# Attention and channel mixing on one Trainium2 core: statistics of the first x tiles ahead of the transposes' copies, and products placed in a wait for a load

## The chip, the cores and the metric

The kernel runs on one core of a Trainium2 chip. The metric is the time of one execution on the device, in microseconds (us); lower is better. Whole times are medians of several runs, with the lowest and highest in brackets where they are given; everything read from a trace is one execution. Engine names in the profile: PE is the matmul engine (TensorE), PEld its weight loads, DVE is VectorE, ACT is ScalarE, POOL is GpSimd, SP the queue that issues most transfers.

## The reference

```python
# batch 8, heads 8, seq 576, head_dim 64, 32 memory slots, d_model 512
a = exp(phi - max(phi, axis=seq));  a = a / (sum(a, axis=seq) + 1e-9)
k_m = einsum('bhsm,bhsd->bhmd', a, k)
v_m = einsum('bhsm,bhsd->bhmd', a, v)
attn = softmax(q @ k_m.T / sqrt(64))            # over the 32 slots
x = (attn @ v_m) laid out as [batch, seq, 512]
xn = (x - mean(x)) / sqrt(var(x) + 1e-6) * g
out = x + relu(xn @ w1) @ w2                    # w1 512x2048, w2 2048x512
```

## The kernel before

Batches are worked off one after the other, and two batches form a pair of 1152 rows, which gives nine tiles of 128 rows. The step of an even batch finishes four of them (`t[0]` to `t[3]`), that of an odd batch five. A step begins with the hidden layer of batch b (`mm1`, tile `h_ps`), then runs the second product tile by tile (`mm2`, tile `ch_ps`, two halves of 8 matmuls per tile), and between those halves it does the attention of the next batch: `a_kv` (memory keys and values), `a_tr` (their transposes), `a_sc` (scores), `a_w1b`, `a_den`. The accumulators lie in PSUM, in two kinds of buffers:

```python
def big(shape, dtype, name):      # two banks each
    return psum.tile(shape, dtype, name=name, tag="big", bufs=3)

def one(shape, dtype, name):      # one bank each
    return psum.tile(shape, dtype, name=name, tag="one", bufs=2)
```

The functions that the change moves:

```python
def x_stats(pr, t):               # VectorE: mean and variance of one x tile
    ...
    nc.vector.bn_stats(out=stt, in_=x)
    nc.vector.bn_aggr(out=mv[:, i, :], in_=stt)

def x_rstd(pr, ts):               # ScalarE: 1/sqrt(var + eps) as Ln and Exp
    ...
    nc.scalar.activation(out=rstd[:, 0:n], in_=mv[:, 0:n, 1], func=AF.Ln, bias=eps_sb)
    nc.scalar.activation(out=rstd[:, 0:n], in_=rstd[:, 0:n], func=AF.Exp, scale=-0.5)

def mm2(pr, t, j0, j1, ...):      # PE: products of one tile into a one-bank buffer
    if j0 == 0:
        chs[(pr, t)] = one([P, C], FP32, "ch_ps")
    ...

def mm2_out(pr, t):               # VectorE: x = ch * rstd + x, frees that buffer; then two writes
    nc.vector.scalar_tensor_tensor(out=x, in0=ch_ps, scalar=rstd, in1=x,
                                   op0=ALU.mult, op1=ALU.add)
    ...
```

The step, cut to what matters (`half(i)` is 8 product matmuls; three tiles in flight need three one-bank buffers, and there are two, so `half(4)`, which opens the third tile, needs `mm2_out(t[0])`):

```python
half(0)
a_kv(nb)                                  # kv_ps; ends with a reciprocal on VectorE (line 232)
x_tiles(pr, t[0:2], False); x_tiles(pr, t[2:4], False)
...
half(1)
a_tr(nb)                                  # kvT: two PSUM copies on VectorE
x_stats(pr, t[0]); x_stats(pr, t[1])
...
half(2)
a_sc(nb)                                  # scores; their exponentials on ScalarE
x_rstd(pr, t[0:2])
a_w1b(nb, 0)                              # evicted by VectorE
mm2_out(pr, t[0])
half(3)
a_den(nb, finish=False)
mm2_out(pr, t[1])
...
half(4)
a_den2(nb)
if odd:
    x_tiles(pr, t[4:5], False)            # fifth tile, four small matmuls
...
```

Batch 1 has a prologue of its own, whose q is transposed on PE in two halves as its load arrives:

```python
mm2(0, 2, 8, 12)
a_tr(1)
a_qT(1, 0)            # 10 transposes into a big buffer, first half of q
a_qT(1, 1)            # 10 transposes, second half of q
a_w1b(1, 0)
mm2(0, 2, 12, 16)     # last four products of tile 2, then mm2_out of tile 2
a_w1b(1, 1)
a_sc(1)
mm2(0, 3, 0, 4)
a_w1b(1, 2)
a_den(1)
...                   # then mm1(1), the first step of the loop
```

The softmax here doesn't subtract the row's maximum and nothing guards it: scores larger than these inputs give would overflow.

## Time and profile before

| | before |
|---|---|
| time, us | 253.18 (253.05 to 253.28, 3 runs) |
| span of the profiled run, us | 251.4 |
| PE busy | 94% |
| idle of PE before `qT_ps` of batch 0 and 1, waiting for the q load | 1.6 us, of which 0.91 in batch 1 |
| idle of PE before `ch_ps`, waiting for `mm2_out` | 1.5 us in six steps |

A timeline row gives the start, the duration, the engine and line, the instruction with its output and input and their shapes, how many were run together, and in brackets the idle time just before it and what ended that. A "releaser" is only the event that came last.

```profile
70.28 1.48 ACT L313 ACTIVATE E_sb<-sc_ps,rs 128x640 bf16<-128x640 f32 x2 [2.30 <-PE sc_ps L308]
71.64 0.29 ACT L445 ACTIVATE rstd<-mv,eps_sb 128x2 f32<-128x2 f32 x1
71.97 0.20 ACT L446 ACTIVATE rstd<-rstd 128x2 f32<-128x2 f32 x1
```

### The profile page before, as it was taken

What the parts mean: (1) busy time and instruction counts of PE and PEld (TensorE: products, weight loads), DVE (VectorE), ACT (ScalarE), POOL (GpSimd) and SP (SyncE); (2) the same over time, 40 slices, a digit from 0 to 9 for tenths busy, and PEclk for the clock granted to TensorE, in tenths of its full rate; (3) what the DMA queues carried; (4) which work ended last, traced back from release to release, by engine and by line L of the source; (5) the groups of instructions that cost most, each with busy time, mean ns of one, the idle gap of its engine ahead of it and who ended that gap; (6) DMA issues with size and microseconds to landing.
All of it is one profiled execution on the core that took longest, in us unless ns stands there. A gap on an engine that the chain in (4) does not pass through costs nothing.

```text
span 251.4 us, 5829 instructions
## 1 busy us (share of the span) xinstructions
PE 236.0 (94%) x2446; PEld 131.6 (52%) x2477; DVE 155.1 (62%) x300; ACT 130.1 (52%) x219; POOL 60.0 (24%) x99
## 2 busy tenths in 40 slices
PE   7878999899999999999999999999999999999993
PEld 2443555447534665367534674467444764476453
DVE  3236773595397655787479646885679537873641
ACT  3154662677364464837382646655581755465220
POOL 8643231027204502090206302270205010000000
PEclk9999999999999999999999999999999999999999
DMA  7999999999996798739973998539892300303133
GB/s 148 192 206 207 206 257 215 282 212 128 211 193 128 130 256 182 146 53 202 249 147 89 142 252 136 123 43 223 200 188 44 78 8 0 86 16 71 44 81 83
DMA packets 41922, 36.82 MB, mean 146 GB/s; under 512 B 17444, under 2 KB 37160, under 8 KB 41896
## 3 DMA queue, kind: packets, MB, share of 16 engines
q0 software_dynamic: 17248, 19.53, 45.8%
q1 hardware_dynamic: 24488, 16.79, 29.2%
q8 instruction: 19, 0.31, 0.5%
q10 hardware_dynamic: 160, 0.13, 0.2%
q14 instruction: 7, 0.06, 0.1%
HBM read 41.42 MB, written 9.44 MB: 202 GB/s over the span
## 4 chain that ended last, share of the span: by engine, by line
PE 72%; DMA 17%; ACT 5%; DVE 2%; issue 2%; POOL 1%; POOLq 0%
PE ch_ps L459 41%; PE h_ps L390 22%; DMA q_bf<-in_q_dram 7%; DMA w2b<-in_moe_w_ch_dram 6%; ACT E_sb L313 4%; DMA kv_bf<-in_k_dram 3%; PE w1b_ps L369 2%; PE o_ps L420 2%; DVE x_sb L483 2%; PE kv_ps L205 2%; PE last_ps L471 1%; PE sc_ps L308 1%; POOL q_bf L92 1%; ACT rstd L446 1%; ACT rstd L445 0%
## 5 line engine op out<-in xcount | busy, mean ns | idle before, releaser
L459 PE MATMUL ch_ps<-w2b,rT 128*128 128x512 bf16 x531 | 123.4, 379 | 3.9 <-issue 1.7
L459 PEld LDWEIGHTS <-rT 128*128 128x128 bf16 x560 | 52.2, 98 | 64.5 <-issue 7.8
L390 PE MATMUL h_ps<-Eh,w1b 128*128 128x288 bf16 x512 | 66.7, 285 | 0.7 <-ACT rT L396 0.5
L396 ACT ACTIVATE rT<-h_ps 128x576 bf16<-128x576 f32 x88 | 52.5, 648 | 27.4 <-PE h_ps L390 27.3
L390 PEld LDWEIGHTS <-w1b 128*128 128x128 bf16 x512 | 49.6, 97 | 17.2 <-issue 2.0
L373 DVE SCALAR_TENSOR_TENSOR w1b<-m_sb,rsum,w1b_ps 128x512 bf16<-128x512 f32 x64 | 43.8, 743 | 6.4 <-PE w1b_ps L369 3.5
L398 DVE TENSOR_SCALAR rT<-h_ps 128x576 bf16<-128x576 f32 x40 | 30.3, 758 | 26.9 <-PE h_ps L390 26.3
L483 DVE SCALAR_TENSOR_TENSOR x_sb<-ch_ps,rstd,x_sb 128x512 f32<-128x512 f32 x35 | 25.6, 744 | 8.6 <-PE ch_ps L459 6.9
L426 ACT ACTIVATE x_sb<-o_ps 128x1024 f32<-128x1024 f32 (+1 forms) x20 | 17.8, 933 | 18.4 <-PE o_ps L420 18.4
L439 DVE BATCH_NORM_STATS2 bst<-x_sb 128x6 f32<-128x512 f32 x36 | 24.3, 676 | 3.1 <-ACT x_sb L426 3.1
L189 POOL TENSOR_TENSOR es<-e_sb 128x512 f32<-128x512 bf16 x6 | 6.9, 1156 | 68.1 <-ACT e_sb L182 68.1
L313 ACT ACTIVATE E_sb<-sc_ps,rs 128x640 bf16<-128x640 f32 x16 | 11.8, 790 | 19.5 <-PE sc_ps L308 19.5
L276 POOL TENSOR_TENSOR vb<-v,vmask 128x256 bf16<-128x256 bf16 x12 | 7.7, 662 | 57.3 <-DVE rs L232 57.3
L445 ACT ACTIVATE rstd<-mv,eps_sb 128x2 f32<-128x2 f32 (+1 forms) x20 | 5.9, 296 | 27.3 <-DVE mv L440 27.3
L355 DVE SCALAR_TENSOR_TENSOR Eh<-E_sb,rs,rden 128x576 bf16<-128x576 bf16 x16 | 12.4, 816 | 8.1 <-ACT rden L354 8.1
L174 PE MATMUL w_ps<-fill 128*128 128x512 f32 x14 | 9.8, 819 | 1.6 <-DVE fill L119 1.6
L369 PE MATMUL w1b_ps<-w1r,kvT 64*32 64x512 bf16 x256 | 10.7, 381 | 0.0
L222 DVE CAST k<-kv_ps 128x256 bf16<-128x256 f32 x7 | 3.0, 424 | 12.5 <-PE kv_ps L205 12.5
L182 ACT ACTIVATE e_sb<-phi_st 128x1152 bf16<-128x1152 f32 x8 | 9.2, 1152 | 2.7 <-DMA phi_st<-in_phi_dram 2.7
L354 ACT ACTIVATE rden<-rden 128x576 f32<-128x576 f32 x16 | 10.0, 673 | 0.1
L261 DVE COPY kvT<-kvT_ps 128x256 bf16<-128x256 bf16 x8 | 2.3, 292 | 12.2 <-PE kvT_ps L259 11.8
L92 POOL DMA_DIRECT2D q_bf<-in_q_dram x10 | 7.6, 761 | 4.6 <-DMA w2b<-in_moe_w_ch_dram 1.9
(73 smaller groups left out, 155.1 us busy)
## 6 DMA issues: line engine op xcount, KB each, us to landing
out_dram<-x_sb SPq DMA_DIRECT2D x70, 128.0 KB, 3.5
kv_bf<-in_k_dram POOLq DMA_DIRECT2D x7, 576.0 KB, 8.8
kv_bf<-in_v_dram POOLq DMA_DIRECT2D x7, 576.0 KB, 12.5
phi_st<-in_phi_dram SPq DMA_DIRECT2D x6, 576.0 KB, 10.5
q_bf<-in_q_dram POOLq DMA_DIRECT2D x6, 576.0 KB, 14.9
w1r<-in_moe_w_ch_dram POOLq DMA_DIRECT2D x4, 512.0 KB, 14.2
w2b<-in_moe_w_ch_dram POOLq DMA_DIRECT2D x4, 512.0 KB, 18.8
q_bf<-in_q_dram POOLq DMA_DIRECT2D x4, 288.0 KB, 12.7
```

The lines of the kernel that those rows point to most:

```text
L92: nc.gpsimd.dma_start(out=t.rearrange("p j n x -> p j (n x)")[:, js, 0:NS * D], in_=rows(q, b)[:, js, :])
L313: nc.scalar.activation(out=E_[:, g].rearrange("p (a x) -> p a x", a=2), in_=sc[:, :, 0:HP], func=AF.Exp, scale=s["rs"][:, g:g + 1])
L355: nc.vector.scalar_tensor_tensor(out=Eh[:, g, :], in0=s["E"][:, g, 0:S], scalar=s["rs"][:, g:g + 1], in1=rd[:, g].rearrange("p a x -> p (a ...
L369: nc.tensor.matmul(ps[32 * j:32 * (j + 1), g, :], s["kvT"][r:r + 64, 2, 32 * j:32 * (j + 1)], w1r[r:r + 64, j, fs], start=True, stop=True, ...
L373: nc.vector.scalar_tensor_tensor(out=s["w1b"][:, g, fs], in0=m_sb[:, fs], scalar=s["rsum"][:, g:g + 1], in1=ps[:, g, :], op0=ALU.mult, op1 ...
L390: nc.tensor.matmul(h_ps[:, half, 0:HS], s["w1b"][:, g, P * j:P * (j + 1)], s["Eh"][:, g, HS * half:HS * (half + 1)], start=(g == 0), stop= ...
L396: nc.scalar.activation(out=dst, in_=h_ps[:, :, 0:HS], func=AF.Relu)
L398: nc.vector.tensor_scalar(out=dst, in0=h_ps[:, :, 0:HS], scalar1=0.0, scalar2=None, op0=ALU.max)
L426: nc.scalar.activation(out=x[:, 0:n].rearrange("p i (u y) -> p i u y", u=2), in_=o_ps.rearrange("p u (i y) -> p i u y", i=2)[:, 0:n], func ...
L439: nc.vector.bn_stats(out=stt, in_=x)
L459: nc.tensor.matmul(ch_ps, rT[:, j, P * t:P * (t + 1)], w2b[:, j, :], start=(j == 0), stop=(j == JC - 1))
L483: nc.vector.scalar_tensor_tensor(out=x, in0=ch_ps, scalar=rstd, in1=x, op0=ALU.mult, op1=ALU.add)
```

## The change

It wants to free the first tile's product buffer earlier in each step (`x_stats`, `x_rstd` and `mm2_out` of the first tile move forward), to put the fifth tile's small matmuls next to the other small ones, and to give PE work in the wait for q in batch 1. For that last part the second q half is put into two one-bank buffers, copied half by ScalarE and half by VectorE. The whole diff:

```diff
--- before.py
+++ after.py
@@ -287,12 +287,21 @@
             nc.sync.dma_start_transpose(out=qTs[b].rearrange("p j n x -> p (j n) x"),
                                         in_=q_bf.rearrange("p j n x -> p (j n x)"))
             return
-        q_ps = big([P, 2, 1024], BF16, "qT_ps")
+        split = b == 1 and i == 1
+        if split:
+
+            qs = [one([P, 1024], BF16, "qT_ps") for _ in range(2)]
+        else:
+            q_ps = big([P, 2, 1024], BF16, "qT_ps")
+            qs = [q_ps[:, u, :] for u in range(2)]
         for u in range(2):
             for n in range(NP):
-                nc.tensor.transpose(q_ps[:, u, P * n:P * (n + 1)], q_bf[:, 2 * i + u, n, :], ident)
+                nc.tensor.transpose(qs[u][:, P * n:P * (n + 1)], q_bf[:, 2 * i + u, n, :], ident)
         dst = qTs[b][:, 2 * i:2 * i + 2].rearrange("p a n x -> p a (n x)")
-        if i == 0 or b == 1:
+        if split:
+            nc.scalar.activation(out=dst[:, 0], in_=qs[0][:, 0:NP * P], func=AF.Copy)
+            nc.vector.tensor_copy(out=dst[:, 1], in_=qs[1][:, 0:NP * P])
+        elif i == 0 or b == 1:
             nc.scalar.activation(out=dst, in_=q_ps[:, :, 0:NP * P], func=AF.Copy)
         else:
             nc.vector.tensor_copy(out=dst, in_=q_ps[:, :, 0:NP * P])
@@ -555,9 +564,9 @@
     mm2(0, 2, 8, 12)
     a_tr(1)
     a_qT(1, 0)
+    mm2(0, 2, 12, 16)
     a_qT(1, 1)
     a_w1b(1, 0)
-    mm2(0, 2, 12, 16)
     a_w1b(1, 1)
     a_sc(1)
     mm2(0, 3, 0, 4)
@@ -601,23 +610,24 @@
             a_kv(nb)
         x_tiles(pr, t[0:2], False)
         x_tiles(pr, t[2:4], False)
+        if odd:
+            x_tiles(pr, t[4:5], False)
         if nb + 1 < B:
             phis[nb + 1] = load_phi(nb + 1)
             load(nb + 1)
         half(1)
+        x_stats(pr, t[0])
+        x_stats(pr, t[1])
+        x_rstd(pr, t[0:2])
         if more:
             a_tr(nb)
-        x_stats(pr, t[0])
-        x_stats(pr, t[1])
         if nb + 1 < B:
             a_qT(nb + 1, 0)
+        mm2_out(pr, t[0])
         half(2)
         if more:
             a_sc(nb)
-        x_rstd(pr, t[0:2])
-        if more:
             a_w1b(nb, 0)
-        mm2_out(pr, t[0])
         half(3)
         if more:
             a_den(nb, finish=False)
@@ -629,9 +639,7 @@
         half(4)
         if more:
             a_den2(nb)
-        if odd:
-            x_tiles(pr, t[4:5], False)
-        else:
+        if not odd:
             a_w1b(nb, 1)
             a_w1b(nb, 2)
             a_w1b(nb, 3)
```

After the change, lines from the second q half on have numbers that are 9 higher: the product is line 468 instead of 459, `mm2_out` 492 instead of 483, `w1b`'s eviction 382 instead of 373.

## The prediction

> **What bounds the kernel now.** I read the page's busy table first, then the waits of the matmul engine, then its timeline beside those of the weight loads and of VectorE.
>
> ```profile
> PE 236.0 (94%) x2446; PEld 131.6 (52%) x2477; DVE 155.1 (62%) x300; ACT 130.1 (52%) x219; POOL 60.0 (24%) x99
> PE ch_ps L459 <- issue: 1.7, 11, 0.2
> PE qT_ps L293 <- DMA q_bf<-in_q_dram: 1.6, 2, 0.9
> ...
> PE ch_ps L459 <- DVE x_sb L483: 1.5, 6, 0.3
> ```
>
> PE is the bound. The waits view (what waited, for whom, us in total, times, longest) lists about 10 us of PE waiting in all, so no reordering of other engines can give much. The change aims at two lines: the q wait of batch 1 (0.91 us, the longest of its two) and the six waits for line 483, `mm2_out`. The "issue" line is not time to win: its 11 gaps of 0.16 us stand where a run of 8 matmuls shows only 7 records, so a record is missing.
>
> Next, one odd step (b=1), PE, then weight loads, then VectorE (start, duration, instruction, idle before and its releaser):
>
> ```profile
> 65.46 0.75 PE L420 MATMUL o_ps<-vb,Eh 64*64 64x128 bf16 x20
> ...
> 72.32 0.44 PE L339 MATMUL den_ps<-E_sb,blk 64*64 64x288 bf16 x8
> 73.01 0.59 PE L459 MATMUL ch_ps<-w2b,rT 128*128 128x512 bf16 x2 [0.25 <-DVE x_sb L483]
> ```
>
> ```profile
> 72.69 0.10 PEld L459 LDWEIGHTS <-rT 128*128 128x128 bf16 x1 [0.23 <-issue]
> 73.01 0.96 PEld L459 LDWEIGHTS <-rT 128*128 128x128 bf16 x5 [0.23 <-issue]
> ```
>
> ```profile
> 66.12 0.16 DVE L232 RECIPROCAL rs<-kv_ps 128x2 f32<-128x2 f32 x1
> 68.25 0.29 DVE L261 COPY kvT<-kvT_ps 128x256 bf16<-128x256 bf16 x1 [1.97 <-PE kvT_ps L259]
> ...
> 70.63 1.41 DVE L373 SCALAR_TENSOR_TENSOR w1b<-m_sb,rsum,w1b_ps 128x512 bf16<-128x512 f32 x2
> 72.20 1.41 DVE L483 SCALAR_TENSOR_TENSOR x_sb<-ch_ps,rstd,x_sb 128x512 f32<-128x512 f32 x2 [0.17 <-ACT rstd L446]
> ```
>
> The third tile's product needs the PSUM bank of the first tile, and VectorE frees it only at 72.20 + 0.75 = 72.95. The weights were loaded at 72.69, and the matmul starts at 73.01. Where nothing is awaited, the first matmul starts with its weight load (70.48 and 70.49 in the same step). So the wait costs 73.01 - 72.69 = 0.32 us, a little more than the printed 0.25, since modelled matmul ends overlap. VectorE is late only because of its order: it sat idle for 1.97 us before the kvT copy, while the statistics, which could have run then, came after it.
>
> **What the Trainium skill says.** "TensorE: Matmul & The Clock Gate", in Architectural detail, says that PE can pull weight loads ahead of matmuls in flight, and that ACT and DVE are strict FIFO. The trace agrees on both: the load at 72.69 ahead of its matmul, and the idle 1.97 us with ready work behind. "Perfetto Trace Analysis", Identifying the Most-Contended Engine, warns that busy share of matmuls is a poor measure; I therefore use starts, not busy time. "TensorE: Matmul & The Clock Gate", Back-to-back issue gap, gives N/2.4 + 2.5, about 216 ns for 512 columns; the trace agrees (8 products take 1.73 us on the chain of waits, 0.216 each). "PSUM — Partial Sum Buffer", Terms, has 8 banks. Here 3 two-bank tiles and 2 one-bank tiles use all of them, so any new allocation waits for an older one.
>
> **Part 1, statistics first (steps b=1 to 6).** Nothing is added, VectorE and ScalarE are reordered. New VectorE order, by durations of the rows above: first x tile evicted at 66.03 + 1.02 = 67.05; two statistics with aggregates, 68.86 to 70.54 before, so 1.69 us: done 68.8. kvT copies (0.29 + 0.28, overlapping) done by 69.3. PE needs kvT at 69.87, so the copies, though later by 0.7 us, still make it with 0.5 us to spare. ScalarE has the reciprocal deviations by 69.4, `mm2_out` of tile 0 ends near 70.2, and the bank is free 2.5 us early. The next waits there (scores' Exp, den, the later w1b buffers) are set by PE's own earlier work; in even steps the third w1b buffer comes free at about 104.3, and PE would arrive at 104.46. So the whole wait goes: 6 x 0.32 = **-1.9 us**.
>
> **Part 2, the fifth tile's `x_tiles` moves up (odd steps).** Its 4 matmuls cost 75.05 - 74.73 = 0.32 us where they stand now, between two products (last product starts 74.52, the next would at 74.73), because of the switch to and from a quarter-array shape. Beside the other o_ps matmuls they cost about 0.14 us. But the built program shows a new wait: as fourth big PSUM tile in a row they take the slot of kv_ps, and wait for the reciprocal of line 232. That ends at 66.28, plus 0.05 for the release = 66.33, against 66.0 for the last o_ps matmul. So the next product starts at 66.33 + 0.07 + 0.14 = 66.55, where it now starts at 66.16: +0.39 there, -0.32 at the old place, **+0.07** in b=1, 3 and 5. The last step has no kv_ps: **-0.17**. Sum about 0.0.
>
> **Part 3, the prologue of batch 1.** Four products (4 x 0.216 = 0.86 us) go into the 0.91 us q wait, which looks like -0.9. I do not believe it, by two terms:
>
> ```profile
> 46.66 0.73 PE L293 MATMUL qT_ps<-ident,q_bf 128*128 128x128 bf16 x10 [0.91 <-DMA q_bf<-in_q_dram]
> 47.32 0.41 PE L369 MATMUL w1b_ps<-w1r,kvT 64*32 64x512 bf16 x8
> 47.66 1.04 PE L459 MATMUL ch_ps<-w2b,rT 128*128 128x512 bf16 x4
> 48.63 0.41 PE L369 MATMUL w1b_ps<-w1r,kvT 64*32 64x512 bf16 x8
> 48.86 0.74 PE L308 MATMUL sc_ps<-qT,kvT 64*32 64x320 bf16 x16
> 49.75 0.59 PE L459 MATMUL ch_ps<-w2b,rT 128*128 128x512 bf16 x2 [0.16 <-issue]
> ```
>
> ```profile
> 47.80 1.41 DVE L373 SCALAR_TENSOR_TENSOR w1b<-m_sb,rsum,w1b_ps 128x512 bf16<-128x512 f32 x2 [2.02 <-PE w1b_ps L369]
> ```
>
> First, the second one-bank q tile takes the bank of the very product that was moved. The four products start at 45.59 and their result is complete at about 46.66; line 483 takes 0.75, so the bank is free at 47.41 and the last five transposes start at 47.46, not 47.0. Second, the second score tile waits, before as after, for the eviction of the first w1b buffer: now 47.80 + 1.41 = 49.21, and the weight loads of the second score tile start at 49.26. VectorE is therefore the path here, not PE. After, VectorE copies the q half (estimate 0.5 us from 0.82 for twice the size) from 47.95 to 48.45, and evicts w1b from 48.37 to 49.77. The second score tile starts at 49.83 instead of 49.27, **+0.56**. From there PE has the same work left; it recovers some 0.15 us, since its wait before the second den tile (for the second w1b eviction) disappears, and gives part back in the first h_ps, which needs Eh, itself 0.5 later. Net **+0.45 us**, with -0.3 to +0.7 thinkable.
>
> **Sum**: -1.9 + 0.0 + 0.45 = -1.4 us; 253.18 - 1.4 = **251.8 us**, -0.6%.
>
> **The rivals.** (a) The intent holds in full: -0.9 in the prologue, -1.9 in the steps, -0.5 from tile five without a new wait: 249.9 us. Against it: the two PSUM slots above, which the built program's waits name. (b) The statistics delay kvT so that scores wait, a wait in the place of the one removed: it needs the 0.5 us margin to be eaten in the odd steps, where ScalarE's third eviction also queues. Since statistics need only the first eviction, I think it unlikely; 0.2 us in each of six steps would make it 253.0. (c) DMA takes the gain: the loads of a batch are issued a step ahead, and the waits view has only 0.2 us for kv_bf in PE's matmuls, so a PE that is 0.3 us faster in each step of 26 to 30 us does not catch up with them. (d) The prologue costs more than 0.7 us because the q half lands later; then 252.3.
>
> **Range and chances.** The repeats of before spread by 0.23 us. The steps' gain is the surest term, 1.5 (six times the printed 0.25) to 1.9; the prologue and part 2 carry some 0.5 us each way. 251.0 to 252.7 should hold 8 times in 10. A 2% move is 5 us, half of all PE waits listed, and in the other direction nothing comes near: same 0.985, faster 0.01, slower 0.005.
>
> **What would show it.** PE's waits for line 483 before the third tile are gone, the first product after den starts with its weight load, and the period of an even step (84.73 to 110.47, 25.74 us) drops to about 25.4, of an odd one (29.64) to about 29.4. A new PE wait of 0.1 to 0.3 us for VectorE's line 232 stands at the fifth tile in three odd steps. In the prologue PE waits near 47.0 for line 483 (instead of 46.6 for DMA), and again about 1 us before the second score tile; the first h_ps of b=1 starts near 55.0, not 54.52. Wrong would be: kvT waits in the steps, or a first h_ps before 54.3.

## More of the kernel before

ScalarE was idle for 2.30 us until the scores came. It then did the two exponentials of the scores and only after them the two tiny instructions of the reciprocal deviation (`rstd`), which therefore was ready at 72.17. VectorE's `mm2_out` needs it.

## The result, and the profile after

| | before | after |
|---|---|---|
| time, us, same rounds | 253.23 (253.05 to 253.74, 4 runs) | 251.38 (251.06 to 251.78, 4 runs) |
| span of the profiled run, us | 251.4 | 249.8 |

The ratio is 0.9925, with a 95% interval of 0.9902 to 0.9947. Ratios in this document are the mean time of one kernel's fast runs over the mean of the other's fast runs of the same rounds, so they are not quite the ratio of the medians. The change gains 0.75%, which is within 2%.

PE is still the bound. The table of busy times, and two lines of the waits view (what waited, for whom, us in total, times, longest), of the kernel after:

```profile
PE 235.2 (94%) x2446; PEld 131.8 (53%) x2477; DVE 155.9 (62%) x301; ACT 130.4 (52%) x219; POOL 60.2 (24%) x99
PE sc_ps L317 <- DVE w1b L382: 1.0, 1, 1.0
PE qT_ps L299 <- DMA q_bf<-in_q_dram: 0.5, 2, 0.3
```

The six waits of a product for `mm2_out` are gone from the list. The q wait has shrunk from 0.91 to 0.28 us in batch 1. In its place stands a wait that was not in the list before: 1.01 us of the scores for a `w1b` eviction.

**The steps.** I measure a step from the first `h_ps` matmul of one batch to that of the next. In the seven stretches every kernel below repeats its figure to some 0.05 us, unless it is named, while whole times spread by 0.5 us and more:

| us | b=1 | b=2 | b=3 | b=4 | b=5 | b=6 | b=7 to the last product |
|---|---|---|---|---|---|---|---|
| before | 30.05 | 25.74 | 29.64 | 25.74 | 29.64 | 25.74 | 22.88 |
| after | 29.90 | 25.43 | 29.43 | 25.43 | 29.43 | 25.43 | 22.67 |

The even steps gain 0.31, the odd ones 0.21 (the first 0.15), the last 0.21. The sum is 0.15 + 2 x 0.21 + 3 x 0.31 + 0.21 = 1.71 us. The first `h_ps` came at 54.66 instead of 54.52, 0.14 later. 1.71 - 0.14 = 1.57 us is the difference of the two profiled spans (1.6).

The timeline of the first step after the change, first the weight loads, then VectorE, then ScalarE, to be laid beside those of before:

```profile
66.55 0.11 PEld L429 LDWEIGHTS <-Eh 64*128 64x128 bf16 x4 [0.30 <-DVE rs L232]
...
73.31 2.70 PEld L468 LDWEIGHTS <-rT 128*128 128x128 bf16 x14 [0.23 <-issue]
```

```profile
67.30 0.69 DVE L448 BATCH_NORM_STATS2 bst<-x_sb 128x6 f32<-128x512 f32 x1 [0.81 <-ACT x_sb L435]
...
69.60 0.75 DVE L492 SCALAR_TENSOR_TENSOR x_sb<-ch_ps,rstd,x_sb 128x512 f32<-128x512 f32 x1
```

```profile
69.04 0.29 ACT L454 ACTIVATE rstd<-mv,eps_sb 128x2 f32<-128x2 f32 x1 [0.37 <-DVE mv L449]
...
70.89 1.48 ACT L322 ACTIVATE E_sb<-sc_ps,rs 128x640 bf16<-128x640 f32 x2 [1.32 <-PE sc_ps L317]
```

The loads of the third tile's products run on in one row of 14 from 73.31: the hole between 72.69 and 73.01 of before is closed. `mm2_out` starts at 69.60 and frees the buffer at 70.35, about 3 us before it is needed (72.95 before, when PE stood waiting). ScalarE now does `rstd` in the idle time ahead of the scores' exponentials. The first row is the price of part 2: the fifth tile's matmuls wait for VectorE's line 232, as forecast. From the first `o_ps` matmul to the first score it now takes 70.49 - 65.67 = 4.82 us, before 69.87 - 65.46 = 4.41.

**The prologue of batch 1.** PE's timeline after the change:

```profile
45.34 1.03 PE L468 MATMUL ch_ps<-w2b,rT 128*128 128x512 bf16 x4
46.65 1.00 PE L299 MATMUL qT_ps<-ident,q_bf 128*128 128x128 bf16 x10 [0.28 <-DMA q_bf<-in_q_dram]
...
49.55 0.33 PE L317 MATMUL sc_ps<-qT,kvT 64*32 64x320 bf16 x8 [1.01 <-DVE w1b L382]
...
54.66 1.09 PE L399 MATMUL h_ps<-Eh,w1b 128*128 128x288 bf16 x7
```

Ten transposes took 1.00 us here, where the same ten took 0.73 before: the first five started at 46.65 and the other five at 47.21, 0.56 later, when `mm2_out` had given back the bank (it ran from 46.41 to 47.16). Then the second score tile waits 1.01 us. So nothing is left of the 0.91 us of wait that was filled: with these waits the first `h_ps` comes 0.14 us later than before.

### The profile page after: what moved, and what is told of

Read it like the earlier page. It is cut to its first block, busy times and chain, and to the rows that moved or that the text cites. A ratio compares the mean times of both kernels' runs of the same rounds, so it can differ in the third digit from the quotient of the medians.

```text
span 249.8 us, 5829 instructions
## 1 busy us (share of the span) xinstructions
PE 235.2 (94%) x2446; PEld 131.8 (53%) x2477; DVE 155.9 (62%) x301; ACT 130.4 (52%) x219; POOL 60.2 (24%) x99
## 4 chain that ended last, share of the span: by engine, by line
PE 85%; DMA 6%; POOL 3%; DVE 2%; issue 2%; ACT 1%; POOLq 0%
PE ch_ps L468 48%; PE h_ps L399 25%; DMA w1r<-in_moe_w_ch_dram 6%; PE w1b_ps L378 3%; PE kv_ps L205 2%; PE o_ps L429 2%; PE last_ps L480 1%; DVE w1b L382 1%; POOL kv_bf L84 1%; PE sc_ps L317 1%; PE den_ps L348 1%; POOL w1r L137 1%; POOL q_bf L92 1%; PE m_ps L164 1%; ACT rT L405 1%
## 5 line engine op out<-in xcount | busy, mean ns | idle before, releaser
L492 DVE SCALAR_TENSOR_TENSOR x_sb<-ch_ps,rstd,x_sb 128x512 f32<-128x512 f32 x35 | 26.1, 746 | 10.7 <-PE ch_ps L468 7.6
L205 PE MATMUL kv_ps<-kv_bf,e_sb 64*32 64x128 bf16 (+1 forms) x648 | 7.4, 215 | 0.6 <-DMA kv_bf<-in_v_dram 0.3
```

What stands on the lines that cost most here:

```text
L205: nc.tensor.matmul(ps[32 * j:32 * (j + 1), g, 0:D * (sl.stop - sl.start)], e[r:r + TS, c, j, :], kv[r:r + TS, j, sl, D * c:D * (c + 1)], s ...
```

## The experiments

Twelve runs were made, in four groups, each group on one chip with its own runs of the kernel before. One run of the kernel before in the second group (261.61 us, at a granted clock of 0.979) was slow and is not counted. In the last column is the time from the first transpose of the second q half (PE starts it as soon as its load is in, but in e11 and e12 as soon as the moved products are through, see below) to the first `h_ps` of batch 1, from the starts in the trace.

| run | what it is | us | ratio to before (95%) | q to h_ps, us |
|---|---|---|---|---|
| (before) | | 253.2 | 1 | 7.86 |
| (after, first rounds) | whole change | 251.38 | 0.9925 (0.9902 to 0.9947) | 8.01 |
| e1_steps | before + part 1 | 251.59 | 0.9934 (0.9922 to 0.9946) | 7.86 |
| e2_fifth | before + part 2 | 253.53 | 1.0011 (0.9998 to 1.0024) | 7.86 |
| e3_prologue | before + part 3 | 253.72 | 1.0021 (1.0007 to 1.0034) | 8.17 |
| e4_big_slot | change, second q half in a big buffer | 251.56 | 0.9931 (0.9919 to 0.9943) | 7.71 |
| e5_stats | before + statistics alone | 253.31 | 1.0011 (0.9985 to 1.0037) | 7.86 |
| e6_stats_rstd | e5 + `x_rstd` | 251.59 | 0.9929 (0.9913 to 0.9945) | 7.86 |
| e7_scores_first | change, prologue in another order | 251.97 | 0.9954 (0.9936 to 0.9972) | 7.27 |
| e8_fifth_after_den | change, fifth tile after den | 251.15 | 0.9919 (0.9903 to 0.9935) | 8.38 |
| e10_slot_and_den | e4 and e8 together | 250.86 | 0.9904 (0.9884 to 0.9924) | 7.71 |
| e11_change_again | whole change | 252.45 | 0.9982 (0.9952 to 1.0012) | 8.45 |
| e12_change_third | whole change | 252.37 | 0.9967 (0.9948 to 0.9986) | 8.45 |
| e13_repairs_again | e4 and e8 together | 250.88 | 0.9910 (0.9894 to 0.9925) | 7.71 |

My theory was the sum of the prediction: the steps gain all, the fifth tile nothing, the prologue loses some. The rival was the intent of the change: each part gains, the prologue most.

### The three parts alone

e1 takes part 1 alone:

```diff
         half(1)
-        if more:
-            a_tr(nb)
         x_stats(pr, t[0])
         x_stats(pr, t[1])
+        x_rstd(pr, t[0:2])
+        if more:
+            a_tr(nb)
         ...
+        mm2_out(pr, t[0])
         half(2)
         if more:
             a_sc(nb)
-        x_rstd(pr, t[0:2])
-        if more:
             a_w1b(nb, 0)
-        mm2_out(pr, t[0])
```

> The kernel before with the statistics, the reciprocal deviations and the first mm2_out of each step moved ahead, and nothing else of the change. Theory (the wait for the first tile's bank was 0.32 us in each of six steps and vanishes): 1.9 us below the kernel before (1.5 to 2.1), all PE waits for the line of mm2_out gone, even steps 25.43 us and odd steps about 29.3 us long. Rival (the gain of the whole change is mostly from the prologue or the fifth tile, or the kvT copies that now come later make the scores wait): under 0.8 us, with a PE wait for kvT in the steps.

Measured: 251.59 us against 253.24 (252.94 to 253.61, 11 runs), so 1.65 less. Each of the six steps is 0.31 shorter than before (29.74, 25.43, 29.33 and so on), the last stays at 22.88, and no PE wait for `mm2_out` is listed. 6 x 0.31 = 1.86. The interval of part 1 alone (0.9922 to 0.9946) lies within that of the whole change in its first rounds (0.9902 to 0.9947): part 1 makes practically the whole gain.

e2 takes part 2 alone, the move of the fifth tile's `x_tiles`:

```diff
         x_tiles(pr, t[2:4], False)
+        if odd:
+            x_tiles(pr, t[4:5], False)
 ...
-        if odd:
-            x_tiles(pr, t[4:5], False)
-        else:
+        if not odd:
             a_w1b(nb, 1)
```

> The kernel before with only the x_tiles of the fifth tile moved up in the odd steps. Theory (0.32 us of shape switches saved at the old place, 0.39 us spent at the new one because the slot of kv_ps is awaited, 0.17 us saved in the last step): within 0.3 us of the kernel before, weight loads of the fifth tile waiting about 0.3 us for the reciprocal of line 232 in three steps. Rival (no new wait, the move saves a switch in four steps): 0.6 to 0.8 us below.

Measured: 253.53 us, 0.3 above before, with an interval that just includes no difference. The traces are sharper: odd steps grow by 0.09 (30.14 and 29.73 for 30.05 and 29.64), even ones stay, and the last stretch falls by 0.21 to 22.67. 3 x 0.09 - 0.21 = +0.06 us. This part is worth nothing.

e3 takes part 3 alone: the q half in two one-bank buffers, and this move:

```diff
     a_qT(1, 0)
+    mm2(0, 2, 12, 16)
     a_qT(1, 1)
     a_w1b(1, 0)
-    mm2(0, 2, 12, 16)
```

> The kernel before with only the prologue part: four products in the q wait and the second q half in two one-bank tiles. Theory (VectorE, which now evicts the product and copies a q half before it evicts the first w1b buffer, makes the second score tile wait): 0.2 to 0.6 us above the kernel before; the stretch from the last kv_ps matmul to the first h_ps of batch 1 about 0.35 us longer. Rival (the products fill the q wait): 0.5 to 0.9 us below.

Measured: 253.72 us, 0.5 above before, and its interval (1.0007 to 1.0034) excludes a gain. The trace has 8.17 instead of 7.86 us from the q load to `h_ps`, and 0.06 more in the first step (30.11). The intent, a gain of 0.9 us, is refuted.

### Which of the moves in part 1 does it

I had written that VectorE was late "only because of its order". If so, it would be enough to move the statistics. e5 does just that, and e6 moves `x_rstd` as well and leaves `mm2_out` behind the `w1b` eviction:

```diff
# e5_stats, against before
         half(1)
-        if more:
-            a_tr(nb)
         x_stats(pr, t[0])
         x_stats(pr, t[1])
+        if more:
+            a_tr(nb)
# e6_stats_rstd, in addition
         x_stats(pr, t[1])
+        x_rstd(pr, t[0:2])
         if more:
             a_tr(nb)
 ...
             a_sc(nb)
-        x_rstd(pr, t[0:2])
-        if more:
             a_w1b(nb, 0)
         mm2_out(pr, t[0])
```

> The kernel before with only the two statistics of each step moved ahead of the kvT copies; the reciprocal deviations stay behind the scores' Exp on ScalarE and the first mm2_out behind the w1b eviction on VectorE. Theory (ScalarE's place for the reciprocal deviations is what held mm2_out: they ended at 72.17 in the step looked at, behind an Exp that PE's scores release): same as the kernel before within 0.3 us, six PE waits for the line of mm2_out as before, steps 25.74 and 29.64 us. Rival (the statistics' place on VectorE was the delay, as the prediction said): 1 to 1.9 us below.

> As the last, and the reciprocal deviations moved ahead of the scores' Exp too; only the first mm2_out stays behind the w1b eviction on VectorE. Theory: the deviations are early, VectorE goes from the w1b eviction straight to mm2_out, at 71.96 instead of 72.20, so each step gains about 0.25 of the 0.32 us: 1.3 to 1.6 us below the kernel before, odd steps 29.40 and even steps 25.50 us. Rival (the place of mm2_out behind the w1b eviction was the delay): within 0.4 us of the kernel before.

Measured: e5 takes 253.31 us like before (253.22 in the same rounds without its slow run), and all its stretches are those of before. e6 takes 251.59, and its steps are 0.25 to 0.27 us shorter. ScalarE's timeline in the first step of e5, with VectorE's `mm2_out` and the line of the waits view below it:

```profile
70.57 1.48 ACT L313 ACTIVATE E_sb<-sc_ps,rs 128x640 bf16<-128x640 f32 x2 [2.30 <-PE sc_ps L308]
71.94 0.29 ACT L445 ACTIVATE rstd<-mv,eps_sb 128x2 f32<-128x2 f32 x1
```

```profile
72.50 1.41 DVE L483 SCALAR_TENSOR_TENSOR x_sb<-ch_ps,rstd,x_sb 128x512 f32<-128x512 f32 x2 [0.17 <-ACT rstd L446]
PE ch_ps L459 <- DVE x_sb L483: 1.5, 6, 0.3
```

The statistics were ready before the scores, but `rstd` still queues behind the exponentials on ScalarE, so `mm2_out` starts as late as before and all six waits remain. In e6 the two `rstd` instructions come ahead:

```profile
68.96 0.30 ACT L445 ACTIVATE rstd<-mv,eps_sb 128x2 f32<-128x2 f32 x1 [0.86 <-DVE mv L440]
70.40 1.48 ACT L313 ACTIVATE E_sb<-sc_ps,rs 128x640 bf16<-128x640 f32 x2 [0.91 <-PE sc_ps L308]
```

So of the 0.31 us of a step, 0.25 to 0.27 come from `rstd`'s place in ScalarE's queue (with the statistics, which it needs, ahead of it), and the other 0.05 from `mm2_out` ahead of the `w1b` eviction. The fourth combination, `rstd` moved and the statistics left behind, was not run. In the trace of before the statistics end at 70.36 + 0.18 = 70.54, after the scores had come (70.28), so it is not shown that ScalarE's order alone would do: e5 shows only that VectorE's order of the statistics alone does not.

### The prologue: the buffer or the order

e4 keeps the whole change, but puts the second q half into a two-bank buffer again, copied by ScalarE alone:

```diff
-        split = b == 1 and i == 1
+        split = False
```

> The whole change, but the second q half stays in a two-bank tile and is copied by ScalarE in one piece. Theory (the one-bank tiles cost: they wait for the moved product's eviction and put a copy on VectorE ahead of the w1b eviction): 0.3 to 0.5 us below the whole change, that is 2.0 to 2.4 us below the kernel before; the second score tile starts about 0.3 to 0.6 us earlier, but still waits for VectorE's w1b eviction. Rival (the split copy is what the move needs, as the scores wait for a 1.24 us copy): 0.3 us or more above the whole change.

Measured: 251.56 us, a ratio of 0.9931, which is not below the whole change's 0.9925 of the first rounds: as a difference of totals the expectation failed. Those two were not in the same rounds, and the load came late in e4's trace (46.94 instead of 46.65). From the load to `h_ps` it took 7.71 us, 0.30 less than in the change's trace, as expected. The repeats below (e10, e13) show the 7.71 us again, but together with e8's edit, so what the big buffer alone is worth in the total was not measured in the same rounds.

e7 takes the big buffer with both engines copying, scores right after the first `w1b`, and the last `w1b` put into the hidden layer of batch 1:

```diff
-    a_w1b(1, 1)
     a_sc(1)
     mm2(0, 3, 0, 4)
-    a_w1b(1, 2)
+    a_w1b(1, 1)
     a_den(1)
 ...
-    a_w1b(1, 3)
+    a_w1b(1, 2)
 ...
-    late = []
+    late = [lambda: a_w1b(1, 3)]
```

> The whole change with another prologue: the second q half in a two-bank tile, copied by ScalarE and VectorE at once, the scores right after the first w1b part, and the later w1b parts behind them, the last inside the first product of batch 1. Theory (VectorE's w1b evictions are the path from the arrival of q to the first h_ps, because the second score tile waits for one of them; without that wait den comes about 1 us earlier): from the first transpose of the second q half to the first h_ps 6.8 to 7.3 us, where the whole change has 8.0 and the kernel before 7.9; step 1 then 0.3 us longer; 0.4 to 0.9 us below the whole change, 2.1 to 2.7 below the kernel before. Rival (VectorE's total work in that stretch is the bound, so order does not matter): within 0.3 us of the whole change.

Measured: 251.97 us. The prologue fell to 7.27 us as expected, but the first step grew to 30.77, by 0.87 instead of the 0.3 that I had allowed, so the total missed its forecast (2.1 to 2.7 us below before; it is 1.25 below 253.22). Its timeline, PE and then VectorE:

```profile
56.68 0.41 PE L374 MATMUL w1b_ps<-w1r,kvT 64*32 64x512 bf16 x8
57.02 1.23 PE L395 MATMUL h_ps<-Eh,w1b 128*128 128x288 bf16 x8
58.42 5.19 PE L395 MATMUL h_ps<-Eh,w1b 128*128 128x288 bf16 x40 [0.18 <-ACT rT L401]
```

```profile
57.46 1.40 DVE L378 SCALAR_TENSOR_TENSOR w1b<-m_sb,rsum,w1b_ps 128x512 bf16<-128x512 f32 x2
```

The moved `w1b` matmuls take PE 0.34 us (56.68 to 57.02), which was allowed for. But the eight `h_ps` matmuls behind them take 1.40 us (57.02 to 58.42), where in the change 56 of them take 7.19 us from their start to that of the next product (56.12 to 63.31), so eight 1.03, and a wait for an eviction of `h_ps` ends that stretch. The `w1b` tile holds one of the three big buffers until VectorE has evicted it, at 57.46 + 1.40 = 58.86, so that only two are left to `h_ps`; that this is the reason of the wait is read from the rows and was not tested. The gain of the prologue (7.27 against the change's 8.01, 0.74 us) was given back in the next stage.

### The fifth tile

e8 puts the fifth tile's matmuls right behind the other small matmuls that stand late in the step, those of den (the trace's `64*64`, a quarter of the array; the fifth tile's are `64*128`, half of it), in the steps 1, 3 and 5, and leaves them early in the last step:

```diff
-        if odd:
+        if last:
             x_tiles(pr, t[4:5], False)
 ...
             a_den(nb, finish=False)
+            if odd:
+                x_tiles(pr, t[4:5], False)
         mm2_out(pr, t[1])
```

> The whole change, but the x_tiles of the fifth tile stands right after den in steps 1, 3 and 5 (in the last step it stays up). Theory (up there it waits about 0.25 us for the slot of kv_ps; beside den it finds a free slot and needs no shape switch of its own): odd steps 29.15 to 29.2 us instead of 29.43, no weight load waiting for line 232 there: 0.7 to 0.9 us below the whole change, 2.4 to 2.8 below the kernel before. Rival (the slot wait is hidden, or the eviction on ScalarE after den delays Eh): odd steps 29.4 us or more.

Measured: 251.15 us, 2.07 below before (253.22), where 2.4 to 2.8 was expected; the odd steps are 29.23 us, 0.20 below the change's 29.43, and the last stretch stays at 22.67. PEld's timeline of the first step in e8:

```profile
73.32 0.14 PEld L348 LDWEIGHTS <-blk 64*64 64x64 bf16 x8 [0.42 <-issue]
73.69 0.12 PEld L429 LDWEIGHTS <-Eh 64*128 64x128 bf16 x4 [0.23 <-issue]
73.91 2.06 PEld L468 LDWEIGHTS <-rT 128*128 128x128 bf16 x11
```

From den to the next product it takes 73.91 - 73.32 = 0.59 us, against 73.31 - 72.94 = 0.37 in the change without the tile in between: the four matmuls cost 0.22 us there, where they cost 0.32 between two products (by the prediction's working, from the trace of before), and 0.41 next to the other `o_ps` (4.82 - 4.41). The differences 0.10 and 0.20 are those of the step lengths.

### Both repairs, and the change again

e10 and e13 are one kernel, the change with e4's and e8's edits together. e11 and e12 are the change itself, run beside them.

> The whole change with both repairs: the second q half in a two-bank tile copied by ScalarE, and the fifth tile right after den in steps 1, 3 and 5. Theory (each removes a PSUM slot wait that the change brought): from the second q half's first transpose to the first h_ps 7.71 us as in the run with the two-bank tile alone, odd steps 29.23 us as in the run with the fifth tile alone; 0.6 to 1.2 us below the whole change run in the same rounds. Rival (what the repairs give is lost to the arrival of the loads in the prologue): within 0.3 us of the whole change.

> The whole change once more, for comparison in the same rounds. Theory (the steps are fixed to a few hundredths of a us, and what varies between runs is when the loads of the prologue arrive): step periods 25.43 and 29.43 us as before, total 251.1 to 251.9 us; the stretch from the second q half to the first h_ps between 8.0 and 8.4 us, longer where PE comes late to the moved product.

> The whole change a third time, since its first two comparisons gave 0.9925 and 0.9982. Theory (the steps gain 1.7 us in every execution, and the prologue costs 2.02 us less the time between the first transposes of the two q halves, which the arrival of the load sets): in the trace, the first h_ps of batch 1 comes 9.88 us after the first transpose of the first q half whatever the load does (7.86 us after the second half's in the kernel before); steps 25.43 and 29.43 us; total 251.2 to 252.4 us, ratio 0.993 to 0.997. Rival (the second comparison was another chip's steady behaviour of the steps): steps longer than 25.5 and 29.6 us.

> The version with both repairs once more beside it. Theory: 7.71 us from the second q half's first transpose to the first h_ps, steps 25.43 and 29.23 us; 0.7 to 1.6 us below the whole change in the same rounds, 2.0 to 2.6 below the kernel before.

Measured: with both repairs 250.86 (250.74 to 251.38, 4 runs) and 250.88 (250.69 to 251.00, 4 runs); the change beside them 252.45 (252.06 to 254.77, 6 runs) and 252.37 (251.47 to 253.24, 6 runs). Twice, on two chips, the repairs take 1.5 to 1.6 us off the change. The traces of e12 and e13 show 8.45 - 7.71 = 0.74 of it in the prologue and 3 x 0.20 = 0.60 in the odd steps. Two forecasts of totals missed: e11 was expected at 251.1 to 251.9, and e10 0.6 to 1.2 below e11. PE's prologue in e12, then in e13:

```profile
46.66 0.44 PE L299 MATMUL qT_ps<-ident,q_bf 128*128 128x128 bf16 x5
47.66 0.44 PE L299 MATMUL qT_ps<-ident,q_bf 128*128 128x128 bf16 x5 [0.56 <-DVE x_sb L492]
...
50.00 0.33 PE L317 MATMUL sc_ps<-qT,kvT 64*32 64x320 bf16 x8 [1.00 <-DVE w1b L382]
```

```profile
46.71 0.73 PE L299 MATMUL qT_ps<-ident,q_bf 128*128 128x128 bf16 x10
...
49.32 0.33 PE L317 MATMUL sc_ps<-qT,kvT 64*32 64x320 bf16 x8 [0.22 <-DVE w1b L382]
54.42 1.21 PE L399 MATMUL h_ps<-Eh,w1b 128*128 128x288 bf16 x8
```

With the one-bank buffers the second five transposes wait for `mm2_out`, here for 0.56 us; with the big buffer ten follow each other in 0.73 us. The last transposes start at 47.66 in e12 though their load had landed at 46.3, before that of e13 (46.7).

The traces also give a rule for that. In all five traces with part 3 as it was written, the first `h_ps` comes 9.87 to 9.89 us after the first transpose of the *first* q half, whenever the load of the second half arrives: the path runs through the four moved products and their `mm2_out` (transposes of the second five 2.43 to 2.44 us after, `h_ps` 7.44 to 7.45 us after these). For e12 the 9.88 us were forecast before it ran.

In the traces with the old prologue it comes 7.86 us after the second half. So the part costs 9.88 - 7.86 = 2.02 us minus the distance at which the old order would have started the second half, which its load sets. Where PE waited for the load, the starts of the transposes give that distance: 1.88 us in the first trace of the change, 1.46 to 1.94 in the others. In e11 and e12 it did not wait: their 1.42 us is the ten transposes and four products themselves (10 x 0.057 + 4 x 0.216 = 1.43), and the load was in before, at about 46.5 and 46.3 (issued at 28.3, landed 18.2 and 18.0 us later, by the `--tile q_bf` view). In the traces where PE waits, transposes start 0.04 to 0.05 us after the landing; so the old order could have started about 1.3 and 1.1 us after the first half there. That makes the loss 0.1 to 0.6 us where PE waited and about 0.7 and 0.9 in e11 and e12 (an estimate from these numbers, and no old-order trace has such an early load), and never a gain.

The sum for the repairs: six steps -1.86; the fifth tile 3 x (0.09 - 0.20) - 0.21 = -0.54; prologue 7.71 - 7.86 = -0.15, and +0.06 in the first step, as in e3. Together -2.49; measured, by medians, -2.32 and -2.27, some 0.2 less.

## Why the prediction was right

- **The total.** The prediction was 251.8 us with 251.0 to 252.7; the medians of the change in its three sets of rounds are 251.38, 252.45 and 252.37. All lie in the range, and "same within 2%" holds in each. The spread between them is larger than I had thought from the 0.23 us of the repeats.
- **The steps.** Predicted 0.32 us in each of six, measured 0.31 (e1). The working, bank free at 70.2 and PE needing it 2.5 us later, held: it was free at 70.35 in the change's trace, about 3 us early. No new wait for kvT arose (one of 0.4 us is listed before and after), so rival (b) fell. The loads did not catch up with PE in the steps either: the periods repeat to some 0.05 us in all traces but one, so rival (c) fell.
- **What held `mm2_out`.** Here a step of the reasoning was wrong: "VectorE is late only because of its order." e5 changed VectorE's order of the statistics and gained nothing; e6 shows that ScalarE's order was the reason, `rstd` behind the exponentials. The row that the prediction quoted said so already: its `mm2_out` ends a wait "[0.17 <-ACT rstd L446]". The size came out right because the change moved both. VectorE's order, `mm2_out` behind the `w1b` eviction, accounts for 0.05 of the 0.31.
- **The buffers.** The eight banks of "PSUM — Partial Sum Buffer", Terms, led me to look for which buffer each moved tile takes. Both forecast waits are in the trace: 0.30 us for line 232 at the fifth tile, and the second five transposes for `mm2_out`. The Trainium skill adds in "Perfetto Trace Analysis", Optimization Strategy, that the same gap repeating on the engine that should be saturated can mean that PSUM lacks room for the next tile. This agrees: the six gaps of about 0.25 us before the third tile were exactly that, and they closed when a buffer was freed earlier.
- **The fifth tile.** Predicted +0.07 per odd step and -0.17 in the last, measured +0.09 and -0.21 (e2). Rival (a), a gain of 0.5 us from it, fell. A reading was wrong: the prediction calls these matmuls quarter-array, but their rows in the trace say `64*128`, half of the array. That the 0.32 us is due to a change of shape was argued; what the runs show is its price at each place.
- **The prologue.** Predicted +0.45, by two terms: the bank of the moved product, and the w1b eviction. Both waits are there, the second of 1.01 us as forecast. The size was right for the spacing of that trace: the rule above gives 2.02 - 1.64 = 0.38 us there (45.02 and 46.66). But I gave it as a constant, and it depends on how early the first half is transposed against the arrival of the second: 0.15 us in the first trace of the change, 0.59 in two others by the transposes' starts, and there 0.7 and 0.9 by the landing of the load. That its variation left the total inside the range is in part luck. Rival (d), more than 0.7 us because the q half lands later, had the direction reversed: a later load makes the filling cheaper.

What stays open: the whole change gained 1.85 us by medians in its first rounds and 0.7 to 0.8 in two later sets. An earlier load of the second q half would explain it: a gain of 1.71 in the steps, less the 0.9 of e12's prologue, leaves 0.8, where the first trace has 1.57. e12's profiled span (250.3) is 1.1 us below the kernel before's (251.4), but before's load landed 0.3 us later than e12's (46.61 against 46.30). In e11 a run of products in the first step had one stall of 0.37 us with no recorded wait, which makes that step 30.26, and its span is 250.6. Each trace shows one execution, and no run changed the load's arrival on purpose, so that the prologue explains the difference of the medians is an inference. The cause of the stall is open.

## What to carry to other kernels

When a wait names an engine, go one step further and ask what that engine's instruction was itself waiting for: the small instruction that must move may stand in another engine's queue. Work put into a wait for a load is only free if what follows the wait does not need the buffer that this work holds; look at which buffer each new or moved tile takes before counting the gain. Where totals spread more than the terms, measure the parts from starts of the same instruction in the traces, and repeat the comparison on another chip before believing a difference of 0.3%.

## What the Trainium skill lacked or had wrong

- "TensorE: Matmul & The Clock Gate", Part 4: PE-mode transpose, gives about 275 ns for a transpose of 128x128 bf16 in a kernel's context, 390 ns in isolation, and says that the full rate of the clock does not engage for it. Here, in the midst of other matmuls, ten in a row take 0.73 us in all; one has a modelled duration of 0.219 us, so the others follow at (0.73 - 0.219)/9 = 0.057 us. The page's own N/2.4 + 2.5 for a warm clock gives 56 ns for 128 columns, which fits the full rate. A series of transposes must be counted by spacing, not by duration.
- The same page's Back-to-back issue gap calls N/2.4 + 2.5 (216 ns for 512 columns) the gap of an isolated matmul and gives about 131 ns for a sustained stream. The runs do not show that: 8 products in a row take 1.73 us, 0.216 each. The prediction says that the trace agrees with the formula, and passes over the 131.
- "TensorEngine Tiling (Array Packing)", Key Properties, says that a change of tiling mode drains TensorE (no run here separates the drain), but I found no page with its price. The runs show four small matmuls at four places: 0.32 us between two products, 0.22 behind den, 0.11 beside their likes in the last step (0.32 - 0.21), and 0.41 beside their likes where the buffer was not free.
- "Perfetto Trace Analysis", Optimization Strategy, advises finding the gaps of the engine to be sped up, what blocks it, and how to make that start sooner. It does not say to put the same question to the blocking instruction, which was needed here: the blocking instruction on VectorE was itself held by ScalarE (e5 against e6: 253.31 and 251.59 us).
- No page that I read says how far a wait can be filled ahead of a load. Here, by the rule worked out above, it would have paid only if the second half could start more than 2.02 us after the first half's transposes did, and by its load it could start 1.1 to 1.9 us after.
